# Attention with decay and a gated convolution FFN: the cleaning of q and k for half batches 4 to 7 on GpSimd instead of VectorE

## The chip, the cores and the metric

The kernel runs on one core of a Trainium2 chip. The metric is the device time of one execution in microseconds; the time before is the median of three runs. The core has TensorE (PE), with its weight loads shown as an engine of their own (PEld), VectorE (DVE), ScalarE (ACT), GpSimd (POOL) and SyncE (SP), whose queue (SPq in the profile) issues nearly all DMAs of this kernel.

## The reference, cut to what matters

Eight batches of eight heads, sequence 576, head size 64; attention with a decay per position, then a gated convolution FFN of width 1024.

```python
scores = q @ k.T / 8                       # per batch and head
cum    = cumsum(log(clip(f, 1e-4, 1)))
scores = where(causal, -1e9, scores + cum[:, None] - cum[None, :])
x      = softmax(scores) @ v               # heads side by side: 8 x 576 x 512
h      = relu(x @ w_in)                    # 8 x 576 x 1024
conv   = sum over k of conv_w[k] * h shifted by k - 1
out    = (h * sigmoid(conv)) @ w_out
```

## The kernel before, in words

The work is cut in 16 half batches (hb) of four heads each, and in 8 batches (b) for the FFN. q and k are wanted with the head size on partitions. They are loaded as 16-bit halves of the 32-bit numbers, so that 64 float32 give 128 partitions of bfloat16: the odd partitions hold the upper halves, which are the bfloat16 values wanted, and the even ones hold the lower halves, which have to be overwritten. For half batches 0 and 1 TensorE turns a plain load; from 2 on a transposing DMA from SP's queue does it (`load_qk`, L224, the DMA on L227), one for q and one for k, each 128x2304 in a ring of four tiles `qk`.

For half batches 2 to 7 a *clamp* cleans the tile in place (`clamp`, L231, the instruction on L233): each element, read as uint16, is multiplied by a factor of its partition (1 on odd, 0 on even ones) and a constant of its partition is added, which puts a bfloat16 1 or -1 or a zero in the rows that serve the decay. Then `rows_of` (L246, DMAs on L249 and L250, from SP's queue) writes the rows of cumulated decay into even partitions 0, 2 and 4, and TensorE can make the scores. From half batch 8 on DMAs (`fill`, L240) do all of it and no clamp is needed.

The scores of a half batch are made in PSUM by TensorE (L359, with the decay riding on the even rows), ScalarE takes the exponentials (L400, L417, L379), TensorE multiplies with v (L436, L441), VectorE divides by the sums (`norm`: L449, L450, reading PSUM), TensorE turns the result (L458, L459) and VectorE or ScalarE copies it out of PSUM (L464). In the FFN of a batch, per block of 128 channels: TensorE (L473), ScalarE's relu (L483), two scalar_tensor_tensor of VectorE for the convolution (L488, L490), ScalarE's tanh (L493), VectorE's gate, a third scalar_tensor_tensor (L497); then TensorE's second matmul (L504, L508), a copy out of PSUM (L514, L519) and the store (L525, L530, L534). GpSimd casts part of v (`cast_v`, L264 and L266) and of the weights (L552), issues a few DMAs for constants (`zc`, L330 and L331) and masks the exponentials of half batches 8 to 15 (L382, L403).

All tasks have names, and the order is written out by hand in one long string, ORDER: `Plan.play` emits the tasks in that order, and every engine and every queue works through its own in that order. Names: `q5.0` is the load of q for half batch 5 (`.1` is k), `cl5.0` its clamp, `rw5` the two row DMAs, `sd`, `so`, `st` scores, `ed`, `eo`, `et` exponentials, `pv` the product with v, `n` norm, `t` and `tx` the turn and its copy, `va` the cast of v, `wo1` and `woc1` the load and cast of a quarter of w_out, `f`, `r`, `c`, `d`, `a`, `g`, `o`, `e`, `s` the steps of the FFN; `@` names the engine where a task can run on several. A clamp depends on its load (`q`); `rw` depends on both clamps. Around the change the string reads (before; parts left out):

```python
"... q5.0 so4.1 g0.1 va3.0@DVE q5.1 ... d0.5 cl5.0 a0.2 so7.1 ... cl5.1 n2.0 q4.1 d0.3 va3.1@POOL eo7.0 wo2 rw5 ..."
"... woc2@POOL g0.2 so6.0 cl4.1 eo6.0 q4.0 f0.7 ... q6.0 n3.0 ... cl4.0 rw4 wo3 ... v2.0 ... cl6.0 g0.7 q6.1 ..."
"... woc3@POOL o0.0 g1.0 eo8.0 cl6.1 ... q7.0 cl7.0 v2.4 so8.1 va5.1@POOL ... rw6 q7.1 ... zc ... cl7.1 ... rw7 ..."
```

Of the kernel before, what the change touches and what calls it, by code (L numbers as in the profile page):

```python
# [25 lines left out]
so7.1 ed7 eo7.1 pv2.0 so7.0 va2.1@DVE pv2.1 cl5.1 n2.0 q4.1 d0.3 va3.1@POOL eo7.0 wo2 rw5 so6.1 eo6.1 woc2@POOL g0.2
so6.0 cl4.1 eo6.0 q4.0 f0.7 r0.7 wo0 woc1@ACT pv3.0 a0.3 a0.5 n2.1 t2 q6.0 n3.0 tx2@ACT c0.7 g0.5 pv3.1 n3.1 a0.4 g0.3
sd11 ed11 so11.1 eo11.1 sd10 so10.1 eo10.1 ed10 cl4.0 rw4 wo3 woc0@ACT t3 tx3@DVE f1.0 r1.0 d0.7 a0.7 c0.6 d0.6 a0.6
f1.1 r1.1 f1.2 g0.4 so11.0 c1.0 v2.0 d1.0 sd8 f1.3 g0.6 r1.2 eo11.0 ed8 cl6.0 g0.7 q6.1 v2.2 r1.3 sd9 ed9 c1.3 d1.3
so8.0 v2.1 f1.4 r1.4 c1.4 d1.4 h1 a1.0 woc3@POOL o0.0 g1.0 eo8.0 cl6.1 st5 et5 a1.4 c1.1 g1.4 d1.1 so10.0 eo10.0 f1.5  # L30
a1.3 g1.3 so9.1 eo9.1 v2.3 va5.0@DVE r1.5 c1.5 d1.5 o0.1 e0.0@ACT f1.6 r1.6 f1.7 r1.7 st4 so9.0 eo9.0 a1.1 va4.0@DVE
pv5.0 q7.0 cl7.0 v2.4 so8.1 va5.1@POOL pv5.1 et4 eo8.1 rw6 q7.1 va4.1@ACT n5.0 sd13 v3.0 v3.4 pv4.0 n5.1 pv4.1 ed13 zc
n4.0 n4.1 a1.5 v3.1 so13.1 sd12 eo13.1 cl7.1 ed12 c1.2 t5 so12.0 eo12.0 t4 tx4@ACT tx5@ACT o0.2 q9.0 c1.7 d1.7 so12.1
eo12.1 a1.7 rw7 o0.3 c1.6 e0.1@ACT f2.0 f2.1 d1.2 d1.6 so13.0 a1.2 g1.5 g1.7 r2.0 f2.2 f2.3 r2.1 q8.1 eo13.0 g1.2 c2.0
st7 a1.6 o0.4 r2.3 g1.1 v3.2 v3.3 q9.1 et7 sd15 d2.0 r2.2 h2 c2.1 a2.0 e0.2@DVE so15.0 so15.1 ed15 g1.6 eo15.0 sd14
ed14 so14.0 eo14.0 f2.4 r2.4 f2.5 va6.0@POOL pv6.0 c2.3 d2.3 q8.0 c2.2 g2.0 so14.1 r2.5 o1.0 eo15.1 va7.0@DVE
va7.1@ACT d2.2 c2.4 st6 eo14.1 pv7.0 a2.2 et6 va6.1@DVE n6.0 pv6.1 d2.1 a2.1 d2.4 n7.0 v4.0 fi9 s0.2 v4.1 c2.5 s0.0
v4.4 fi8 q10.0 s0.1 a2.4 v4.3 n6.1 v4.2 g2.2 o1.1 e1.0@ACT pv7.1 sd19 f2.6 f2.7 q11.0 q10.1 g2.4 ed19 n7.1 r2.6 c2.6
d2.6 r2.7 sd18 ed18 t6 q11.1 t7 o1.2 tx6@DVE tx7@ACT a2.6 a2.3 d2.5 a2.5 g2.1 st9 f3.0 et9 g2.3 f3.1 so19.1 c2.7 d2.7
r3.0 r3.1 a2.7 md19 sd17 ed17 o1.3 f3.2 g2.6 g2.5 c3.0 so19.0 eo19.1 e1.1@DVE r3.2 eo19.0 d3.0 c3.2 o1.4 e1.2@DVE s1.2  # L40
c3.1 d3.1 md18 st8 s1.0 g2.7 fi10 so18.0 fi11 et8 f3.3 va9.0@DVE va9.1@ACT md17 s1.1 v5.0 eo18.0 so17.0 so18.1 h3 d3.2
a3.0 r3.3 eo17.0 a3.1 f3.4 f3.5 f3.6 g3.1 v5.3 v5.1 r3.5 g3.0 o2.0 a3.2 g3.2 c3.3 r3.4 r3.6 sd16 f3.7 eo18.1 mt8 ed16
so16.1 eo16.1 r3.7 d3.3 a3.3 c3.4 d3.4 v5.2 c3.7 d3.7 c3.6 so16.0 eo16.0 o2.1 e2.0@ACT a3.4 pv9.0 a3.7 va8.0@ACT
so17.1 q12.0 n9.0 md16 va8.1@ACT q12.1 eo17.1 o2.2 o2.3 e2.1@ACT st10 et10 c3.5 d3.5 d3.6 mt9 g3.4 pv9.1 n9.1 mt10
pv8.0 pv8.1 a3.5 n8.0 a3.6 n8.1 o2.4 g3.7 q13.0 g3.5 v5.4 e2.2@ACT fi12 s2.2 sd22 ed22 sd20 ed20 md22 t8 tx8@DVE t9
tx9@DVE g3.6 g3.3 q13.1 so20.0 md20 sd23 so22.1 eo20.0 ed23 sd21 md23 va11.0@DVE ed21 f4.0 r4.0 c4.0 d4.0 f4.1 f4.2
r4.1 eo22.1 f4.3 c4.1 r4.2 r4.3 so23.1 eo23.1 h4 so21.1 d4.1 a4.0 g4.0 so23.0 f4.4 r4.4 eo21.1 c4.2 a4.1 s2.1 o3.0
eo23.0 f4.5 v6.0 r4.5 f4.6 d4.2 a4.2 so22.0 md21 g4.1 fi13 eo22.0 c4.4 va11.1@DVE st11 et11 s2.0 mt11 o3.1 c4.5 d4.5
v6.3 so21.0 r4.6 o3.2 v6.1 v6.2 a4.5 so20.1 q14.1 q14.0 eo21.0 e3.0@ACT d4.4 f4.7 eo20.1 c4.6 g4.5 r4.7 sd24 a4.4
pv11.0 ed24 sd25 o3.3 c4.3 d4.3 g4.2 c4.7 d4.7 so25.1 md24 n11.0 pv11.1 ed25 e3.1@ACT va10.0@POOL eo25.1 a4.7 pv10.0  # L50
st12 d4.6 va10.1@POOL pv10.1 et12 sd27 n11.1 n10.0 n10.1 ed27 g4.7 o3.4 t10 e3.2@ACT a4.6 a4.3 t11 sd26 tx10@DVE
tx11@DVE md27 v6.4 ed26 so25.0 so27.1 g4.6 eo27.1 f5.0 f5.1 so26.0 q15.0 r5.0 c5.0 g4.3 d5.0 eo25.0 r5.1 c5.1 f5.2
so24.0 eo26.0 f5.3 f5.4 r5.2 eo24.0 r5.3 g4.4 o4.0 so26.1 so27.0 h5 a5.0 fi14 d5.1 a5.1 r5.4 eo27.0 c5.3 g5.0 d5.3
eo26.1 c5.4 c5.2 s3.2 q15.1 d5.2 so24.1 d5.4 eo24.1 a5.2 g5.1 va12.0@DVE o4.1 f5.5 st13 et13 va12.1@ACT g5.2 f5.6 md25
mt12 md26 r5.5 c5.5 d5.5 f5.7 r5.6 sd28 e4.0@ACT r5.7 c5.7 ed28 pv12.0 n12.0 so28.1 o4.2 pv12.1 a5.5 g5.5 va13.0@ACT
pv13.0 eo28.1 d5.7 a5.3 mt13 sd29 s3.0 md28 o4.3 va13.1@POOL n12.1 ed29 md29 c5.6 n13.0 fi15 pv13.1 a5.4 g5.4 e4.1@ACT
s4.1 n13.1 sd31 ed31 md31 sd30 t12 ed30 d5.6 md30 t13 o4.4 a5.6 tx12@DVE tx13@DVE so31.0 st14 a5.7 g5.6 g5.3 f6.0 et14
mt14 v7.0 eo31.0 r6.0 c6.0 f6.1 r6.1 c6.1 d6.0 f6.2 r6.2 e4.2@ACT so31.1 eo31.1 f6.3 so29.0 so29.1 g5.7 f6.4 r6.3 c6.2
d6.1 d6.2 eo29.0 r6.4 v7.2 c6.4 eo29.1 d6.4 o5.0 so28.0 o5.1 s4.0 h6 a6.1 eo28.0 g6.1 a6.2 st15 f6.5 v7.3 a6.0
e5.0@ACT et15 mt15 s3.1 c6.3 v7.1 va14.0@DVE pv14.0 v7.4 so30.0 s4.2 g6.0 g6.2 r6.5 va15.0@POOL va15.1@ACT eo30.0  # L60
n14.0 so30.1 c6.5 eo30.1 f6.6 r6.6 f6.7 va14.1@POOL pv14.1 d6.5 a6.4 d6.3 n14.1 a6.3 pv15.0 pv15.1 t14 r6.7 c6.6 a6.5
o5.2 n15.0 n15.1 t15 tx14@ACT tx15@ACT c6.7 d6.7 a6.7 d6.6 o5.3 g6.3 g6.7 e5.1@ACT f7.0 f7.1 r7.0 f7.2 o5.4 g6.4 f7.3
g6.5 a6.6 r7.1 c7.0 d7.0 r7.2 e5.2@ACT r7.3 c7.1 d7.1 h7 a7.0 g6.6 c7.2 d7.2 f7.4 f7.5 f7.6 f7.7 g7.0 a7.1 g7.1 r7.6
r7.4 s5.2 o6.0 o6.1 o7.0.0 c7.6 c7.3 r7.5 d7.3 d7.6 a7.2 c7.4 d7.4 a7.3 e6.0@ACT s5.0 g7.3 c7.5 a7.4 g7.2 o6.2 o6.3
o6.4 r7.7 c7.7 d7.5 g7.4 s6.0 o7.2.0 o7.3.0 o7.0.1 o7.0.2 a7.6 o7.2.1 o7.1.0 o7.2.2 e6.1@ACT d7.7 o7.2.3 s5.1 o7.1.1
o7.3.1 o7.1.2 o7.1.3 e6.2@ACT o7.0.3 o7.1.4 o7.2.4 a7.5 g7.6 g7.5 o7.2.5 a7.7 s6.2 s6.1 g7.7 o7.1.5 o7.2.6 o7.2.7
e7.2@ACT s7.2 o7.0.4 o7.0.5 o7.0.6 o7.0.7 o7.1.6 o7.3.2 o7.1.7 e7.0@ACT s7.0 e7.1@DVE o7.3.3 o7.3.4 o7.3.5 o7.3.6
o7.3.7 e7.3@ACT o7.4.0 o7.4.1 o7.4.2 s7.1 o7.4.3 o7.4.4 o7.4.5 s7.3 o7.4.6 o7.4.7 e7.4@ACT s7.4
"""


# [35 lines left out]
def kernel(  # L107
# [11 lines left out]
    nc = tc.nc  # L119
# [34 lines left out]
    cw = cpool.tile([128, NFF, 3], FP32, name="cw")  # L154
    cwt = cpool.tile([128, NFF, 3], FP32, name="cwt")
# [3 lines left out]
    lim = cpool.tile([128, 4], FP32, name="lim")  # L159
# [33 lines left out]
    add = plan.add  # L193
# [34 lines left out]
            t.bitcast(U16)[:, h0 * S:(h0 + nh) * S],  # L228
            src[hb // 2, HH * (hb % 2) + h0:HH * (hb % 2) + h0 + nh].bitcast(U16).rearrange("h s d2 -> (h s) d2"))

    def clamp(hb, h0, nh, side):  # L231
        t = (stq_t, stk_t)[side][hb % RING].bitcast(U16)[:, h0 * S:(h0 + nh) * S]
        nc.vector.tensor_scalar(t, t, lim[:, 2 * side:2 * side + 1], lim[:, 2 * side + 1:2 * side + 2],  # L233
                                op0=ALU.mult, op1=ALU.add)

    def even_rows(hb, first, n, c0, c1):
        t, width = qk_t[hb % RING], 2 * HS + 64
# [50 lines left out]
    for side in range(2):  # L288
# [6 lines left out]
                            op0=ALU.is_equal, op1=ALU.mult)  # L295
# [274 lines left out]
    for hb in range(NHB):  # L570
# [146 lines left out]
```

## Time and profile before

| | |
|---|---|
| median of three runs | 249.03 us (248.84 to 250.57) |
| the profiled execution | 250.38 us |
| its span, and what lies around it | 248.4 us, 2.0 us |
| busy: PE, VectorE, ScalarE, GpSimd | 232.6, 215.3, 213.0, 46.2 us |
| L233 on VectorE | 12 times, 10.5 us, 874 ns each, from 17.7 to 85.3 us |
| L488, L490, L497 on VectorE | 64 times each, mean 832, 852, 806 ns |
| granted TensorE clock | 0.999 |

Busy time is a union of the instructions of an engine. Consecutive instructions overlap a little in the records: a VectorE instruction of 0.87 us is followed by the next after 0.79 us. A name such as "DVE u L490" is engine, written tile and line; SPq is SyncE's queue, which issues a DMA and then goes on. The chain of waits follows the end of the program back through whatever released each step.

### The profile page before, as it was taken

Reading aid. Unit: us, or ns where it says so; the run is one execution under the profiler, and the core shown is the slowest. Engines: PE = TensorE matmul, PEld = TensorE weight load, DVE = VectorE, ACT = ScalarE, POOL = GpSimd, SP = SyncE. Lnnn points to the kernel's source line nnn. Section 1 sums busy time; section 2 is a strip of 40 time slices with the busy share of each in tenths; the row PEclk is TensorE's granted clock in tenths of the full one; section 3 lists DMA queues with packets and bytes.
Section 4 is the critical chain, followed back from the end, with each engine's and each line's share of the span. In section 5 each row is a group of like instructions: output and inputs, shape, how many; then the busy total and the mean of one; then the engine's idle time right before and its main releaser. Section 6 shows DMA issues by size and latency. Waiting matters only on the chain.

```text
span 248.4 us, 6681 instructions
## 1 busy us (share of the span) xinstructions
PE 232.6 (94%) x2768; PEld 150.9 (61%) x2768; DVE 215.3 (87%) x328; ACT 213.0 (86%) x288; POOL 46.2 (19%) x76
## 2 busy tenths in 40 slices
PE   0999989889999999999999999999999999999993
PEld 0887765556456856666555865587556756755441
DVE  5771577998999989989999999997999999999961
ACT  2868938999999999969999899998999999887642
POOL 8000411101104302011203080046012602000000
PEclk9999999999999999999999999999999999999999
DMA  7989999999998999999999989899970690003345
GB/s 198 302 193 193 239 211 231 186 271 203 247 212 180 235 198 250 268 219 218 218 261 253 216 174 268 224 235 160 220 229 5 163 305 2 3 3 106 129 145 191
DMA packets 114694, 48.22 MB, mean 194 GB/s; under 512 B 104034, under 2 KB 105250, under 8 KB 114664
## 3 DMA queue, kind: packets, MB, share of 16 engines
q1 hardware_dynamic: 114210, 46.92, 85.1%
q8 instruction: 21, 0.34, 0.6%
q0 software_dynamic: 208, 0.51, 0.6%
q10 hardware_dynamic: 246, 0.37, 0.5%
q14 instruction: 9, 0.07, 0.1%
HBM read 21.11 MB, written 10.17 MB: 126 GB/s over the span
## 4 chain that ended last, share of the span: by engine, by line
PE 65%; SPq 9%; DVE 9%; DMA 8%; ACT 3%; issue 3%; ACTq 0%; DVEq 0%
PE ps L504 21%; PE ps L473 19%; PE ps L359 11%; SPq L227 6%; PE ps L436 6%; DMA qk<-in_k_dram 3%; PE ps L508 3%; DVE u L488 3%; DMA qk<-in_q_dram 3%; DVE u L490 2%; DMA u<-in_f_dram 2%; PE ps L458 2%; PE ps L441 2%; DVE hg L497 2%; DVE qk L233 1%
## 5 line engine op out<-in xcount | busy, mean ns | idle before, releaser
L417 ACT ACTIVATE pp<-ps 128x1024 f16<-128x1024 f32 x64 | 65.5, 1044 | 4.9 <-PE ps L359 2.7
L473 PE MATMUL ps<-xt,w_in_f 128*128 128x512 f16 (+1 forms) x512 | 68.2, 286 | 1.0 <-ACT ht L483 0.3
L359 PE MATMUL ps<-qk 128*128 128x128 bf16 (+2 forms) x576 | 63.2, 240 | 1.7 <-DVE xm L450 0.6
L504 PE MATMUL ps<-w_out_f,hg 128*128 128x512 f16 x256 | 59.4, 379 | 0.0
L488 DVE SCALAR_TENSOR_TENSOR u<-ht,cwt 128x576 f32<-128x576 f16 x64 | 52.8, 832 | 2.5 <-ACT ht L483 2.4
L490 DVE SCALAR_TENSOR_TENSOR u<-ht,cwt,u 128x576 f32<-128x576 f16 x64 | 53.7, 852 | 1.4
L473 PEld LDWEIGHTS <-w_in_f 128*128 128x128 f16 x512 | 34.0, 98 | 30.4 <-issue 1.8
L493 ACT ACTIVATE hg<-u,cw 128x576 f16<-128x576 f32 x64 | 48.8, 784 | 2.9 <-DVE u L490 2.9
L497 DVE SCALAR_TENSOR_TENSOR hg<-hg,ht 128x576 f16<-128x576 f16 x64 | 50.3, 806 | 1.1 <-ACT hg L493 0.9
L359 PEld LDWEIGHTS <-qk 128*128 128x128 bf16 x576 | 39.2, 98 | 19.2 <-issue 3.4
L483 ACT ACTIVATE ht<-ps 128x576 f16<-128x576 f32 x64 | 41.2, 668 | 2.9 <-PE ps L473 2.8
L504 PEld LDWEIGHTS <-hg 128*128 128x128 f16 x256 | 24.0, 98 | 25.6 <-issue 0.2
L403 POOL TENSOR_SCALAR_AFFINE_SELECT pp<-pd 128x1024 f16<-128x1024 f32 x16 | 18.5, 1168 | 48.7 <-ACT pd L400 42.9
L450 DVE TENSOR_TENSOR xm<-ps,rc 128x896 f16<-128x896 f32 (+1 forms) x32 | 24.3, 758 | 1.1
L436 PE MATMUL ps<-va,pp 128*128 128x65 f16 x640 | 24.6, 193 | 0.6 <-ACT pp L417 0.4
L436 PEld LDWEIGHTS <-pp 128*128 128x128 f16 x640 | 22.4, 97 | 3.0 <-ACT pp L417 0.7
L400 ACT ACTIVATE pp<-ps 128x1024 f16<-128x1024 f32 x16 | 16.5, 1039 | 4.0 <-PE ps L359 3.0
L514 ACT COPY ob<-ps 128x1024 f32<-128x1024 f32 (+1 forms) x18 | 15.1, 839 | 4.0 <-PE ps L504 3.2
L400 ACT ACTIVATE pd<-ps 128x1024 f32<-128x1024 f32 x16 | 15.9, 1023 | 1.9 <-PE ps L359 1.9
L367 PE MATMUL ps<-mask,ident 128*128 128x512 bf16 (+1 forms) x40 | 14.5, 362 | 0.4 <-ACT xt L464 0.2
L233 DVE TENSOR_SCALAR qk<-qk,lim 128x2304 uint16<-128x2304 uint16 x12 | 10.5, 874 | 3.1 <-DMA qk<-in_q_dram 1.9
L382 POOL TENSOR_SCALAR_AFFINE_SELECT pt<-p 128x256 f16<-128x256 f32 x8 | 4.8, 594 | 38.6 <-ACT p L379 37.0
(88 smaller groups left out, 198.9 us busy)
## 6 DMA issues: line engine op xcount, KB each, us to landing
vf<-in_v_dram SPq DMA_DIRECT2D x32, 256.0 KB, 4.9
out_dram<-ob SPq DMA_DIRECT2D x14, 512.0 KB, 4.7
qk<-blank SPq DMA_DIRECT2D x8, 540.0 KB, 7.2
ob<-in_moe_w_in_dram SPq DMA_DIRECT2D x4, 512.0 KB, 4.8
ob<-in_moe_w_out_dram SPq DMA_DIRECT2D x4, 512.0 KB, 5.1
vf<-in_v_dram SPq DMA_DIRECT2D x8, 128.0 KB, 5.0
out_dram<-ob SPq DMA_DIRECT2D x4, 256.0 KB, 2.1
out_dram<-ob SPq DMA_DIRECT2D x15, 64.0 KB
```

The source lines that it names most:

```text
L359: nc.tensor.matmul(o, tk[:, h * S + k0:h * S + k0 + 128], tq[:, h * S + q0:h * S + q0 + n], start=first, stop=last and not by_matmul(hb, h))
L400: nc.scalar.activation(o, ps_of(f"sd{i}").rearrange("p (s c) -> p s c", s=2), AF.Exp, scale=SCALE)
L417: nc.scalar.activation(pair(i)[:, s, 512:1536], ps_of(f"so{i}.{s}"), AF.Exp, scale=SCALE)
L436: nc.tensor.matmul(ps[:, c:c + D + 1], block(hb, h, m, n), va[:, h, m, 0:D + 1], start=(m == 0), stop=(m == n))
L450: nc.vector.tensor_tensor(xm[:, CUT * D * u:CUT * D * u + nj * k * D].rearrange("p (j x d) -> p j x d", x=k, d=D), got[:, :, :, 0:D], r.un ...
L473: nc.tensor.matmul(ps[:, t0:t1], w_in_f16[:, cc, 128 * ff:128 * (ff + 1)], xt[:, cc, x:x + t1 - t0], start=(cc == 0), stop=(cc == NCC - 1))
L483: nc.scalar.activation(ht_of(b, ff)[:, 1:1 + S], ps_of(f"f{b}.{ff}")[:, 0:S], AF.Relu, scale=0.5)
L488: nc.vector.scalar_tensor_tensor(u, ht[:, 0:S], cwt[:, ff, 0:1], ht[:, 1:1 + S], op0=ALU.mult, op1=ALU.add)
L490: nc.vector.scalar_tensor_tensor(u, ht[:, 2:2 + S], cwt[:, ff, 1:2], u, op0=ALU.mult, op1=ALU.add)
L493: nc.scalar.activation(hg_of(b, ff), u_t[slot[f"c{b}.{ff}", "u"]], AF.Tanh, scale=cw[:, ff, 1:2])
L497: nc.vector.scalar_tensor_tensor(hv, hv, 1.0, ht_of(b, ff)[:, 1:1 + S], op0=ALU.add, op1=ALU.mult)
L504: nc.tensor.matmul(ps[:, 512 * (c % 2):512 * (c % 2 + 1)], hg_of(b, ff)[:, 128 * c:128 * (c + 1)], w_out_f16[:, ff, :], **kw)
```

## The change

The tasks `cl4` to `cl7`, two each, run on GpSimd; `cl2` and `cl3` stay on VectorE. `clamp` gets an engine, the tasks `cl2` to `cl7` may run on either, and eight names in ORDER get `@POOL`. No name changes its place in the string. ORDER is written on one line after the change, so lines of the changed kernel are numbered 50 lower (L233 becomes L183, L249 becomes L199).

```diff
 ORDER = """
-... d0.5 cl5.0 a0.2 so7.1 ed7 eo7.1 pv2.0 so7.0 va2.1@DVE pv2.1 cl5.1 n2.0 q4.1 d0.3 va3.1@POOL ...
+... d0.5 cl5.0@POOL a0.2 so7.1 ed7 eo7.1 pv2.0 so7.0 va2.1@DVE pv2.1 cl5.1@POOL n2.0 q4.1 d0.3 va3.1@POOL ...
...
-    def clamp(hb, h0, nh, side):
+    def clamp(hb, h0, nh, side, e="DVE"):
         t = (stq_t, stk_t)[side][hb % RING].bitcast(U16)[:, h0 * S:(h0 + nh) * S]
-        nc.vector.tensor_scalar(t, t, lim[:, 2 * side:2 * side + 1], lim[:, 2 * side + 1:2 * side + 2],
-                                op0=ALU.mult, op1=ALU.add)
+        (nc.gpsimd if e == "POOL" else nc.vector).tensor_scalar(t, t, lim[:, 2 * side:2 * side + 1], lim[:, 2 * side + 1:2 * side + 2],
+                                                                op0=ALU.mult, op1=ALU.add)
...
-                    add(f"cl{hb}.{side}", "DVE", [f"q{hb}.{side}"], lambda hb=hb, side=side: clamp(hb, 0, 4, side))
+                    add(f"cl{hb}.{side}", "DVE/POOL", [f"q{hb}.{side}"], lambda e, hb=hb, side=side: clamp(hb, 0, 4, side, e))
```

(`cl4.0`, `cl4.1`, `cl6.0`, `cl6.1`, `cl7.0` and `cl7.1` get `@POOL` in the same way.)

In GpSimd's own order the eight clamps stand so: wic2, cl5.0, cl5.1, va3.1, woc2, cl4.1, cl4.0, cl6.0, woc3, cl6.1, cl7.0, va5.1, zc, cl7.1, va6.0, and then as before. The row DMAs `rw4` to `rw7` on SP's queue and the first scores of half batches 4 to 7 on TensorE wait for GpSimd where they waited for VectorE. VectorE loses eight instructions; the order of all other engines' instructions is the same.

## The prediction

> **What bounds the kernel now.** The page comes first: the engines' busy times and the chain that ended last.
>
> ```profile
> PE 232.6 (94%) x2768; PEld 150.9 (61%) x2768; DVE 215.3 (87%) x328; ACT 213.0 (86%) x288; POOL 46.2 (19%) x76
> ...
> PE 65%; SPq 9%; DVE 9%; DMA 8%; ACT 3%; issue 3%; ACTq 0%; DVEq 0%
> ```
>
> On average TensorE is the limit and POOL nearly idle. But the eight moved instructions run between 50.66 and 86.17 us, so that stretch must be read by itself: busy time by window (columns: PE, PEld, DVE, ACT, POOL, granted clock, DMA share, GB/s).
>
> ```profile
> 45.00:50.00 5.00, 3.87 (x42) 2.68 (x42) 4.96 (x8) 5.00 (x8) 0.09 (x1) 1.00 1.21 199
> 50.00:55.00 5.00, 4.01 (x72) 2.90 (x73) 4.97 (x9) 4.99 (x7) 0.00 (x0) 1.00 1.04 250
> ...
> 65.00:70.00 5.00, 4.69 (x46) 2.88 (x44) 4.96 (x7) 5.00 (x9) 1.04 (x1) 1.00 1.10 277
> ...
> 75.00:80.00 5.00, 5.00 (x66) 3.14 (x65) 4.96 (x8) 5.00 (x8) 2.00 (x4) 1.00 0.82 168
> ```
>
> Here VectorE and ScalarE are both full, and PE waits for them up to 75 us; from there PE has no gap. Third, the chain of waits in that stretch (start, us, what).
>
> ```profile
> 49.93 0.81 DVE u L490
> 50.74 0.52 DVE qk L233
> ...
> 53.81 0.55 SPq L250
> 54.36 0.05 issue
> 54.41 6.86 DMA qk<-in_q_dram
> 61.27 0.03 issue
> 61.30 0.46 DVE qk L233
> ...
> 72.74 0.83 DVE u L490
> 73.60 0.78 ACT hg L493
> ```
>
> From 38.4 to 73.6 us the chain is VectorE, but for one transposing load (54.41 to 61.27) on which VectorE waits 0.59 us; then ScalarE to 81.3, then PE to the end. So a microsecond added to VectorE before 73.6 goes to the end whole, while one taken away helps only until ScalarE binds.
>
> Fourth, the timeline of VectorE and GpSimd where they overlap (start, us; VectorE first, GpSimd in the second fence).
>
> ```profile
> 39.21 0.81 DVE L488 SCALAR_TENSOR_TENSOR u<-ht,cwt 128x576 f32<-128x576 f16 x1
> 40.12 1.40 DVE L490 SCALAR_TENSOR_TENSOR u<-ht,cwt,u 128x576 f32<-128x576 f16 x1
> ...
> 67.31 1.62 DVE L497 SCALAR_TENSOR_TENSOR hg<-hg,ht 128x576 f16<-128x576 f16 x1
> ```
> ```profile
> 39.83 1.09 POOL L552 CAST w_in_f<-ob 128x1024 f16<-128x1024 f32 x1 [4.04 <-DMA ob<-in_moe_w_in_dram]
> 44.41 0.68 POOL L266 CAST va<-vf 64x256 f16<-64x256 f32 x1 [3.49 <-DMA vf<-in_v_dram]
> ...
> 67.29 1.04 POOL L552 CAST w_out_f<-ob 128x1024 f16<-128x1024 f32 x1 [9.37 <-DMA ob<-in_moe_w_out_dram]
> ```
>
> These rows decide the forecast. L490 takes 0.82 us elsewhere and 1.40 when it begins under a GpSimd cast; L497 takes 0.75 elsewhere and 1.62 under the cast of 67.29, which ends at 68.33: its own 0.75 starts only at 68.18. The other way round, the cast of 44.41 (0.39 us alone, at 188.89) takes 0.68 because L490 runs until 44.84. So a GpSimd instruction that reads SBUF and a VectorE scalar_tensor_tensor exclude each other: GpSimd gets in 0.15 us before the running VectorE instruction's recorded end, and the next scalar_tensor_tensor starts about 0.2 us before GpSimd's end. VectorE's PSUM readers are free of it: L450 under the cast of 56.88 takes 1.09, as without one (52.71).
>
> **The change, part by part.**
>
> *Removed:* eight VectorE L233 instructions of 0.87 us, 0.79 us from start to next start. Five (cl5.0, cl5.1, cl4.1, cl4.0, cl6.0) stand before the last work of the chain's VectorE part: 5 x 0.79 = 3.95 us. With cl4.0 goes the wait for its load at 61.30, 0.68 us (L497 at 59.95 and its usual spacing of 0.67 give 60.62), and VectorE's 0.19 us wait for PE at 56.72, since VectorE will be later: 0.87 us. In all -4.82 us.
>
> *Added on GpSimd:* eight tensor_scalar on 128x2304 uint16, an operation that this engine does not show. Nearest rows: the 128x1024 cast takes 1.04 us, so by proportion 2.34; from the 64x256 cast (0.39) the slope is 0.846 ns per element, 0.39 + 2048 x 0.000846 = 2.12; the 128x1024 affine_select (1.10) by proportion 2.48. I take 2.34 (same proportion as the larger, single-input cast). Ends: 2.12, and 4.68 if multiply and add each cost a pass.
>
> *Added on VectorE, the exclusion:* a clamp that arrives while scalar_tensor_tensors run back to back holds VectorE 2.34 - 0.28 = 2.06 us (mean of the replay below). Followed by hand from 48.74, with landing times of the loads:
> - cl5.0 lands at 48.74, gets in at 49.01 before L488's end, ends 51.36; L490 (49.20) begins at 51.16: +1.96.
> - cl5.1 (landed 50.62) gets in behind that L490 at 51.83, ends 54.18; the second L490: +2.07.
> - Then va3.1, queued behind cl5.1 on POOL (44.41 before, now 54.65): +0.15 on L266. Its user pv3.1 comes at about 59, so nothing else.
> - woc2 (56.88), which lay under L450, now falls on L490/L497: +0.79.
> - cl4.1 lands at 54.79 but stands behind woc2: 58.43 to 60.78, mostly under L449/L450: +0.16.
> - cl4.0: its load is issued 0.83 us later, since SP's rw5 (L249, 53.40) waits for cl5.1's end at 54.18 instead of 53.35. It lands near 62.1, holds to 64.45, the last L497 before tx2 waits +1.73.
> - cl6.0 (lands near 65.5): +2.06. cl6.1 (near 73.8, since SP's rw4 now waits for 64.45 instead of 62.65, 1.8 us, with wo3, v2, q6.1 and later loads behind it): +2.08.
> Sum 1.96 + 2.07 + 0.15 + 0.79 + 0.16 + 1.73 + 2.06 + 2.08 = +11.00 us.
>
> *After 73.6:* cl7.0 holds about 2.06 more for 2 x 0.79 removed, cl7.1 comes behind zc's DMA issues (78.62 to 82.69) and holds at most 2.06 more for the last 0.79. VectorE is then up to 1.75 us further behind; I cost that at nothing, covered by VectorE's slack against PE after 86 (4.31 of 5 us busy in 90 to 95); without that cover it is +1.7. At best it is nothing: ScalarE and PE, not VectorE, are then the chain. rw6 and rw7 wait for nothing new: cl6.1 and cl7.1 end ahead of SP's shifted queue. POOL's zc (needed by the fill at 98.39) has over 10 us.
>
> *Sum:* 11.00 - 4.82 = **+6.2 us**. The profiled execution took 250.38 (span 248.4 and 1.98 around it), so it would be 256.6; it lies 1.35 above the median 249.03, which would be **255.2**. By the ends of the clamp's price, with 4.85 fully exposed clamps: 2.12 gives 255.2 - 4.85 x 0.22 = 254.1; 4.68 gives 255.2 + 4.85 x 2.34 = 266.5, and near 270 with the covered ones.
>
> A page to weigh: the row of L497 shows all but 0.15 us of a GpSimd cast held. The Trainium skill, SBUF — State Buffer, "Who interferes with whom", says a VectorE instruction with two SBUF inputs and a GpSimd one that reads SBUF take turns on a shared port pair, whichever starts first keeping it for the whole instruction. By its letter each hold would be the full 2.34 and the sum 255.2 + 4.85 x 0.28 = 256.6.
>
> **Rivals.**
> 1. *The clamp is slower on GpSimd* (two operations and a conversion). For: the row is missing. Against: every GpSimd row, even affine_select, is near 1 ns per element. At 3.44 us each (proportion of the cast at 95.68, which takes 1.53 beside VectorE work) 255.2 + 5.9 x 1.10 = 261.7 (cl4.1 loses its cover too); at 4.68, 266 to 270. The Trainium skill, GPSIMD Engine Reference, "Elementwise — side-by-side cycle accounting", gives 1.8 cycles per element at 1.2 GHz as the best case of a plain loop, an estimate of 3.46 us here; the cast row (1024 in 1.04) is faster than that.
> 2. *The holds are covered* (the other side: no change or faster). It decides at a hold where 4.85 h + 1.1 = 4.82, so 0.77 us, a clamp of about 1.05 us: less than half of any POOL row; or if uint16 tensor_scalar does not exclude at all. Then VectorE sheds 4.8 us, but ScalarE, full from 45 to 70, gives only its gaps, 0.3 us up to 80 us (0.31 of it between 70 and 75): 248.7. If other waits vanish too, PE's gaps between 35 and 75 (3.5 us) cap it at 245.5.
> 3. *The wait goes to SP instead* (no exclusion, but rw4 waits): cl4.0 ends 61.27 + 2.34 = 63.61 instead of 62.65 as SP's time, and all loads behind come 1.0 us later: 249.0 + 1.0 = 250.0. For: SP is issuing almost without a gap from 45 to 80. Against: it is less than what VectorE loses.
> 4. *Half absorbed:* VectorE's lateness meets slack between 73.6 and 81 that the single chain doesn't show (PE full from 75): 252.
>
> **How the numbers follow.** Forecast as summed 0.52 (its own range 253 to 259, from 254.1 and 256.6 widened by the uncounted 1.7 and by one hold more or less); slower clamp 0.20; half absorbed 0.13; SP 0.06; covered 0.09. The 8-in-10 range leaves out the covered case (0.09) and the upper half of the slow clamp (0.10): 250 to 265. A measurement here tells about 1% (2.5 us) from no change: slower by more, above 251.5, is 0.52 + 0.20 + 0.10 of the absorbed case = 0.82; faster by over 1% only in the best part of the covered case, 0.04; within 1% the rest, 0.14.
>
> **What would show it.** In the profile after: L183 on POOL x8 near 2.3 us each (lines are 50 lower there); VectorE's three scalar_tensor_tensor groups (832, 852, 806 ns) longer by some 13 us in sum; single ones of 2.8 us next to each clamp; VectorE's busy time up, though it lost 7 us of work; PE's gaps between 50 and 85 grown by about 6 us; after 86 us windows as before. Wrong it would be if those groups keep their means (no exclusion), if L183 on POOL is far from 2.3, or if the chain runs through SP's L199 and POOL instead of VectorE.

## The result and the profile after

The changed kernel takes 258.99 us (median of four runs, 258.65 to 259.24) where the kernel before took 249.80 us in the same comparison (248.84 to 250.58): a ratio of 1.0365 [1.0338, 1.0392], slower by 9.2 us. The forecast was 255.2 with a range of 250 to 265, so the sign and the range hold and the size is 3.8 us short (as a difference 3.0 short, 9.2 instead of 6.2, since the kernel before is at 249.80 here and was at 249.03). The profiled execution took 258.65 us against 250.38. Executions of one kernel below can differ by stretches of 3.41 us or more at half TensorE clock; where that matters they are given one by one with their mean granted clock.

The page first, engines and the chain that ended last.

```profile
PE 234.3 (91%) x2768; PEld 152.0 (59%) x2768; DVE 224.5 (87%) x320; ACT 213.6 (83%) x288; POOL 66.9 (26%) x84
...
PE 68%; DVE 14%; DMA 5%; SPq 4%; ACT 3%; issue 2%; ACTq 0%; DVEq 0%
```

VectorE has eight instructions less and is busy 9.2 us longer; its share of the chain goes from 9% to 14%, that of SP's queue falls from 9% to 4%. The groups of the same page say which instructions grew (busy, mean ns of one, idle before).

```profile
L440 DVE SCALAR_TENSOR_TENSOR u<-ht,cwt,u 128x576 f32<-128x576 f16 x64 | 59.2, 937 | 1.4
...
L438 DVE SCALAR_TENSOR_TENSOR u<-ht,cwt 128x576 f32<-128x576 f16 x64 | 57.3, 903 | 2.6 <-ACT ht L433 2.4
...
L447 DVE SCALAR_TENSOR_TENSOR hg<-hg,ht 128x576 f16<-128x576 f16 x64 | 52.1, 835 | 1.3 <-ACT hg L443 1.1
...
L183 POOL TENSOR_SCALAR qk<-qk,lim 128x2304 uint16<-128x2304 uint16 x8 | 21.0, 2630 | 17.7 <-DMA qk<-in_q_dram 15.8
```

The three scalar_tensor_tensors of the convolution (852, 832, 806 ns before, in this order) are longer by 64 x (85 + 71 + 29) ns = 11.8 us in sum; nothing about them was changed. The clamp's mean of 2630 ns includes waiting for VectorE; one that starts free takes 2.26 us. Single instructions show the hold: VectorE's timeline (start, us), then GpSimd's.

```profile
48.67 3.44 DVE L440 SCALAR_TENSOR_TENSOR u<-ht,cwt,u 128x576 f32<-128x576 f16 x2
52.04 2.19 DVE L216 CAST va<-vf 64x256 f16<-64x256 f32 x1
...
65.87 2.62 DVE L440 SCALAR_TENSOR_TENSOR u<-ht,cwt,u 128x576 f32<-128x576 f16 x1
72.28 2.62 DVE L440 SCALAR_TENSOR_TENSOR u<-ht,cwt,u 128x576 f32<-128x576 f16 x1
...
79.52 2.66 DVE L447 SCALAR_TENSOR_TENSOR hg<-hg,ht 128x576 f16<-128x576 f16 x1
...
85.64 3.10 DVE L438 SCALAR_TENSOR_TENSOR u<-ht,cwt 128x576 f32<-128x576 f16 x1
```
```profile
71.31 2.98 POOL L183 TENSOR_SCALAR qk<-qk,lim 128x2304 uint16<-128x2304 uint16 x1 [1.93 <-DMA qk<-in_k_dram]
...
85.86 2.26 POOL L183 TENSOR_SCALAR qk<-qk,lim 128x2304 uint16<-128x2304 uint16 x1
```

The clamp of 85.86 ends at 88.12; the L438 recorded from 85.64 needs 0.81 and ends at 88.74, so it starts work about 87.93, 0.2 us before the clamp's recorded end. At 52.04 it is not a scalar_tensor_tensor but VectorE's cast of v that is held, 2.19 us instead of 0.28. Summed over VectorE between 46 and 93 us, the time beyond each kind's median is 1.0 us in the kernel before and 14.3 us after. This sum is called *held time* below.

By window (PE, PEld, DVE, ACT, POOL, granted clock, DMA share, GB/s):

```profile
50.00:55.00 5.00, 2.63 (x60) 2.08 (x58) 4.97 (x5) 3.19 (x4) 4.48 (x3) 0.91 1.06 293
55.00:60.00 5.00, 5.00 (x78) 3.52 (x78) 4.02 (x7) 3.81 (x5) 3.97 (x3) 0.75 0.93 179
...
65.00:70.00 5.00, 4.50 (x40) 2.49 (x38) 4.80 (x3) 3.82 (x5) 3.76 (x2) 1.00 1.08 253
70.00:75.00 5.00, 2.76 (x25) 1.69 (x25) 4.94 (x5) 3.68 (x5) 2.98 (x1) 1.00 1.23 220
75.00:80.00 5.00, 3.90 (x29) 2.01 (x27) 4.82 (x7) 4.31 (x7) 1.28 (x1) 1.00 1.04 128
...
85.00:90.00 5.00, 3.59 (x77) 2.68 (x75) 4.96 (x5) 4.60 (x7) 3.09 (x3) 1.00 1.21 229
```

ScalarE was full from 45 to 70 and has gaps now; PE, which had 0.1 us of them from 75 to 95, has them up to 90.3 us; and between 54.06 and 57.47 PE ran at half clock. PE's own shift (the same instruction before and after) tells when the time is lost: about -0.5 us at 46, +2.6 at 55, +3.0 at 62, +5.1 at 67, +6.3 at 73, +6.9 at 79, +8.1 at 82, and +8.3 from 83 (times of before) to the end. The chain of waits in that stretch:

```profile
51.30 0.81 DVE u L440
52.12 2.12 DVE va L216
...
54.28 0.54 PE ps L391 x12
...
79.60 2.58 DVE hg L447
...
85.72 3.04 DVE u L438
...
90.39 1.10 DVE xm L400
...
91.53 0.41 PE ps L386 x8
```

VectorE carries it to 91.5 us, not to 73.6. Two of PE's waits there (window 48 to 92; us in total, times, longest) were not in the forecast:

```profile
PE ps L391 <- DVE va L216: 2.2, 1, 2.2
PE ps L386 <- DVE va L214: 1.7, 2, 1.2
```

A third wait, 2.3 us for ScalarE's relu (L433, PE stands from 69.93 to 72.24), brought no half clock. For GpSimd or a row DMA PE waits nowhere in this window.

### The profile page after: what moved, and what is told of

It is laid out like the page before. It is cut to its first block, busy times and chain, and to the rows that moved or that the text cites. A ratio compares the mean times of both kernels' runs of the same rounds, so it can differ in the third digit from the quotient of the medians.

```text
span 256.9 us, 6686 instructions
## 1 busy us (share of the span) xinstructions
PE 234.3 (91%) x2768; PEld 152.0 (59%) x2768; DVE 224.5 (87%) x320; ACT 213.6 (83%) x288; POOL 66.9 (26%) x84
## 4 chain that ended last, share of the span: by engine, by line
PE 68%; DVE 14%; DMA 5%; SPq 4%; ACT 3%; issue 2%; ACTq 0%; DVEq 0%
PE ps L454 20%; PE ps L423 19%; PE ps L309 12%; PE ps L386 6%; DVE u L438 4%; DVE u L440 4%; DMA qk<-in_k_dram 3%; PE ps L458 3%; PE ps L408 2%; PE ps L391 2%; DVE hg L447 2%; SPq L177 2%; PE ps L163 2%; DMA pd<-in_moe_conv_w_dram 2%; ACT ht L433 1%
## 5 line engine op out<-in xcount | busy, mean ns | idle before, releaser
L309 PE MATMUL ps<-qk 128*128 128x128 bf16 (+2 forms) x576 | 64.5, 242 | 2.0 <-DVE xm L400 0.8
L440 DVE SCALAR_TENSOR_TENSOR u<-ht,cwt,u 128x576 f32<-128x576 f16 x64 | 59.2, 937 | 1.4
L438 DVE SCALAR_TENSOR_TENSOR u<-ht,cwt 128x576 f32<-128x576 f16 x64 | 57.3, 903 | 2.6 <-ACT ht L433 2.4
L447 DVE SCALAR_TENSOR_TENSOR hg<-hg,ht 128x576 f16<-128x576 f16 x64 | 52.1, 835 | 1.3 <-ACT hg L443 1.1
L433 ACT ACTIVATE ht<-ps 128x576 f16<-128x576 f32 x64 | 41.1, 664 | 4.7 <-PE ps L423 3.1
L386 PE MATMUL ps<-va,pp 128*128 128x65 f16 x640 | 24.6, 193 | 2.4 <-DVE va L214 1.7
L183 POOL TENSOR_SCALAR qk<-qk,lim 128x2304 uint16<-128x2304 uint16 x8 | 21.0, 2630 | 17.7 <-DMA qk<-in_q_dram 15.8
L386 PEld LDWEIGHTS <-pp 128*128 128x128 f16 x640 | 22.3, 97 | 5.1 <-DVE va L214 2.1
L400 DVE TENSOR_TENSOR xm<-ps,rc 128x896 f16<-128x896 f32 (+1 forms) x32 | 24.3, 758 | 1.1
```

The source lines that it names most:

```text
L309: nc.tensor.matmul(o, tk[:, h * S + k0:h * S + k0 + 128], tq[:, h * S + q0:h * S + q0 + n], start=first, stop=last and not by_matmul(hb, h))
L386: nc.tensor.matmul(ps[:, c:c + D + 1], block(hb, h, m, n), va[:, h, m, 0:D + 1], start=(m == 0), stop=(m == n))
L400: nc.vector.tensor_tensor(xm[:, CUT * D * u:CUT * D * u + nj * k * D].rearrange("p (j x d) -> p j x d", x=k, d=D), got[:, :, :, 0:D], r.un ...
L433: nc.scalar.activation(ht_of(b, ff)[:, 1:1 + S], ps_of(f"f{b}.{ff}")[:, 0:S], AF.Relu, scale=0.5)
L438: nc.vector.scalar_tensor_tensor(u, ht[:, 0:S], cwt[:, ff, 0:1], ht[:, 1:1 + S], op0=ALU.mult, op1=ALU.add)
L440: nc.vector.scalar_tensor_tensor(u, ht[:, 2:2 + S], cwt[:, ff, 1:2], u, op0=ALU.mult, op1=ALU.add)
```

## The experiments

Three mechanisms could make the 9 us. **A, exclusion:** GpSimd's clamp, which reads SBUF, keeps VectorE out. **B, lateness:** what waits for the clamps, or stands behind them in GpSimd's order, comes later, since 2.26 us on GpSimd replace 0.87 on VectorE. **C, clock:** PE's new gaps bring half clock. Each ratio is to the kernel before, run beside it.

### The same place and the same waits, without reading SBUF

`e1_memset`; a memset of the tile takes the place of GpSimd's clamp, so q and k of half batches 4 to 7 are zero.

```diff
-        (nc.gpsimd if e == "POOL" else nc.vector).tensor_scalar(t, t, ...)
+        if e == "POOL":
+            nc.gpsimd.memset(t, 0)
+        else:
+            nc.vector.tensor_scalar(t, t, ...)
```

> The eight GpSimd clamps become memsets of the same 128x2304 uint16 tile: same place, same waits, about the same length (the 64x1152 memset of before takes 1.13 us, so by proportion 2.26, as against 2.26 for an undisturbed clamp), but nothing is read from SBUF. Left out: the cleaning, so q and k of half batches 4 to 7 are zero. Theory A (a GpSimd instruction that reads SBUF and a two-input VectorE instruction exclude each other): the holds of some 14.8 us are gone, VectorE's three scalar_tensor_tensor groups are back at about 830, 850, 806 ns, and the time is 248 to 250, as before the change. Theory B (the rows and scores wait for a later clamp, on SP's queue and on TensorE): the clamps end no earlier, so the time stays near 259.

Measured 250.95 us, ratio 1.0027 [0.9993, 1.0061]. Groups of its page (lines are 3 higher than after):

```profile
L441 DVE SCALAR_TENSOR_TENSOR u<-ht,cwt 128x576 f32<-128x576 f16 x64 | 53.2, 839 | 3.8 <-ACT ht L436 3.7
L443 DVE SCALAR_TENSOR_TENSOR u<-ht,cwt,u 128x576 f32<-128x576 f16 x64 | 54.3, 862 | 1.4
...
L450 DVE SCALAR_TENSOR_TENSOR hg<-hg,ht 128x576 f16<-128x576 f16 x64 | 49.1, 787 | 1.8 <-ACT hg L446 1.6
...
L184 POOL MEMSET qk<- 128x2304 uint16 x8 | 16.2, 2036 | 19.3 <-ACT pp L370 8.1
```

GpSimd is occupied 2.04 us each time, nearly as long as by the clamp, and the convolution keeps its length. Held time is 2.2 us. So at this length neither the place in the order nor the new wait costs the 9 us; what the clamp does and the memset doesn't is the cause. (The operation differs too, not the read alone; but GpSimd's casts, which read and neither multiply nor add, hold the same instructions.)

`e6_memset_short`; the same bytes zeroed as 1152 float32, so that GpSimd is done in half the time (cleaning left out as before):

```diff
+            nc.gpsimd.memset((stq_t, stk_t)[side][hb % RING].bitcast(FP32)[:, 0:HS // 2], 0.0)
```

> As the run with memsets, but each memset is written as 128x1152 float32 (the same bytes), so about 1.05 instead of 2.03 us. Left out: the cleaning, q and k of half batches 4 to 7 are zero. No hold, hardly any lateness: this shows what the 6.3 us taken from VectorE are worth alone. Rival 2 of the prediction said 248.7 against 249.03, a gain of 0.3 us, since ScalarE is full. If lateness had hidden a real gain in the run with memsets of 2.03 us, this one is 2 to 4 us under the kernel before, 247 to 248.5.

Measured 249.91 us, 0.9973 [0.9956, 0.999]: the memset takes 1.06 us, held time is 1.0 as before the change. Taking the clamps off VectorE and giving back nothing is worth 0.7 us [0.3, 1.1], although it sheds 8 x 0.79 = 6.3 us of VectorE's work. By this run that is about what the change could have brought.

### The exclusion with nobody waiting

`e7_idle_read`; the kernel before, whose VectorE keeps its clamps; GpSimd cleans a spare tile that nothing else uses, at each one's place in GpSimd's order (with no load to wait for, the first starts at 41.75).

```diff
     def clamp(hb, h0, nh, side):
+        if hb >= 4:
+            nc.gpsimd.tensor_scalar(spare, spare, lim[:, 0:1], lim[:, 1:2], op0=ALU.mult, op1=ALU.add)
```

> The kernel before, all clamps on VectorE, and eight tensor_scalar of 128x2304 uint16 added on GpSimd in a spare tile, at the clamps' places in the order; nobody waits for their results. Theory A: about 2 us of hold for each that falls beside two-input instructions, nothing saved in exchange; 8 to 14 us over before, 258 to 264, and longer scalar_tensor_tensor groups. Theory B (only the wait for a late clamp costs): no change, 250 to 251.

Measured 262.62 us, 1.0485 [1.0423, 1.0547] (executions 261.6 to 265.3). From its page:

```profile
L494 DVE SCALAR_TENSOR_TENSOR u<-ht,cwt,u 128x576 f32<-128x576 f16 x64 | 58.9, 933 | 1.4
...
L492 DVE SCALAR_TENSOR_TENSOR u<-ht,cwt 128x576 f32<-128x576 f16 x64 | 55.2, 870 | 2.5 <-ACT ht L487 2.4
...
L501 DVE SCALAR_TENSOR_TENSOR hg<-hg,ht 128x576 f16<-128x576 f16 x64 | 54.2, 868 | 1.0 <-ACT hg L497 0.7
...
L237 POOL TENSOR_SCALAR spare<-spare,lim 128x2304 uint16<-128x2304 uint16 x8 | 24.6, 3077 | 0.4
```

No engine waits for the spare tile, the clamps are where they were, and PE waits for no GpSimd instruction between 40 and 95 us, yet held time is 12.4 us and the kernel 11.9 us longer, with half clock for 3.41 us from 70.20 on, behind a PE gap of 1.97 us. A, with what its gaps bring, makes a loss of this size without B. With e1 beside it, A is shown as the cause from which the rest follows.

`e8_idle_write`; as e7, but GpSimd only writes the spare tile.

```diff
     def clamp(hb, h0, nh, side):
+        if hb >= 4:
+            nc.gpsimd.memset(spare, 0)
```

> The same with eight memsets of the spare tile (2.03 us each) in place of the eight tensor_scalar: GpSimd as busy and its queue as long, but nothing read from SBUF. Theory A: no change, 250 to 251.5, and VectorE's groups keep their means. If it is a busy GpSimd as such or its queue that costs, it is as slow as the run with tensor_scalar.

Executions of 251.25 (clock 0.999), 256.83, 256.88 and 257.68 us (0.993): my expectation of no change holds for one of four. The scalar_tensor_tensors are indeed free (835, 851, 816 ns), but VectorE's clamp is not. Its timeline, then GpSimd's:

```profile
82.22 2.39 DVE L267 CAST va<-vf 128x1024 f16<-128x1024 f32 x1
84.53 2.65 DVE L234 TENSOR_SCALAR qk<-qk,lim 128x2304 uint16<-128x2304 uint16 x1
```
```profile
84.08 2.48 POOL L237 MEMSET spare<- 128x2304 uint16 x1
```

The clamp L234 (0.88 alone) runs to 87.18 because the memset holds it to 86.56. The cast before it (0.69 alone) lies under GpSimd's DMA issues of `zc`, which end at 84.09; why it is held there is not shown. Held time is 6.4 us, 5.2 of them on this cast and three of VectorE's clamps. The clamp of 84.53 and the cast before it delay PE, which stands from 85.84 to 88.50 and has half clock from 88.32 on for 3.41 us. So "write only" is not harmless for every VectorE instruction. It was harmless in e1 for the scalar_tensor_tensors; there too one cast (2.15 us instead of 0.69, under the memset of 80.12 to 82.14) is the exception. The Trainium skill, SBUF — State Buffer, "Who interferes with whom", separates these two: two SBUF inputs contend with a GpSimd instruction that reads, while tensor_scalar and cast in a two-port mode contend with any. Both halves agree with the rows (839 against 903 ns; 2.65 against 0.88 us).

### Half of the change, and one clamp of it

`e3_hb45` keeps cl5.0, cl5.1, cl4.1 and cl4.0 on GpSimd, `e4_hb67` the four of half batches 6 and 7, `e11_cl71` cl7.1 alone.

```diff
-... cl6.0@POOL ... cl6.1@POOL ... cl7.0@POOL ... cl7.1@POOL
+... cl6.0@DVE ... cl6.1@DVE ... cl7.0@DVE ... cl7.1@DVE
```

(e4: the same with cl4 and cl5; e11: seven names with `@DVE`.)

> Only half batches 4 and 5 are cleaned on GpSimd; 6 and 7 stay on VectorE. Theory A, by the holds read in the trace after the change (1.89, 1.91, 0.84 and 1.42 us, less 4 x 0.79 of VectorE work and the 0.9 us wait for a load): +2 to +3, so about 252. Theory B: SP's two late rows (rw5, rw4) are both here, so nearly all of the loss, 257 to 259. Theory C (TensorE's granted clock, 0.91 and 0.75 of full from 50 to 60 us after the change, adds much): the dip is here, and the loss is above 4 us.

> Only half batches 6 and 7 are cleaned on GpSimd. Theory A, by the holds read in the trace after the change (1.80, 1.80, 1.91, 2.29, less 4 x 0.79): +4.6 to +5.5, so about 254.5; the last two alone +2.5, since VectorE has no room behind 73.6 us as I had assumed. Theory B: rw6 and rw7 waited for nothing new, so 250 or less. Theory C: no clock dip from 50 to 60, and what is missing from the sum of both halves is the clock's share.

> One clamp alone on GpSimd: cl7.1, whose load lands at 82.6 while VectorE reads PSUM (L449, L450 from 81.4 to 85.3). Theory A: no hold at all, VectorE sheds 0.79 us, GpSimd's clamp takes its bare 2.26 us; the time is that of before or up to 0.5 us less, 250.2 to 250.8. If a clamp on GpSimd costs wherever it stands, about an eighth of the loss, 1.1 us more.

| | us | ratio | held time | held time added, less VectorE's work removed | time added |
|---|---|---|---|---|---|
| e3 | 252.3 | 1.0074 [1.0045, 1.0102] | 6.4 | 6.42 - 1.01 - 4 x 0.79 = +2.2 | +1.9 |
| e4 | 254.31 | 1.0153 [1.009, 1.0216] | 6.5 | +2.3 | +3.8 |
| all eight | 258.99 | 1.0365 [1.0338, 1.0392] | 14.3 | 14.33 - 1.01 - 8 x 0.79 = +7.0 | +9.2 |
| e11 | 250.63 | 1.001 [0.9989, 1.0031] | 3.6 | | +0.3 |

Each half costs, and the second half, two of whose clamps the forecast put behind the end of VectorE's chain, costs more than the first by the middle values (the intervals just touch). Together they cost 3.5 us more than the sum of the two. 2.4 of these are held time itself (14.33 against 6.42 + 6.50 - 1.01), the rest may be room used only once and the half clock, which neither profile of the halves has. e4's ratio is of its three executions without half clock (253.52, 254.16, 254.46); a fourth took 259.21 (clock 0.993). In e11 the one clamp was to fall on VectorE's readers of PSUM; it came later (85.95) and held an L438 by 1.8 us (86.20, 2.61 long), and still costs nothing that can be measured. PE's shift against the kernel before is 1.0 us ahead of this hold and 0.9 behind it: one hold there fits in VectorE's room.

### Lateness by itself

`e2_memset_twice`; e1 with the memset twice, so GpSimd is occupied 4.1 us for each clamp without reading.

```diff
+            for _ in range(2):
+                nc.gpsimd.memset(t, 0)
```

> As the run with memsets, but each memset is done twice, so a clamp ends some 2.3 us later still, without reading SBUF. Left out: the cleaning. Theory A with rows that have room: 249 to 251, for only what SP's queue waits at rw5 and rw4 is added, and it is taken up by gaps. Theory B: each late clamp costs, so the time is well above the run with single memsets, by 4 us or more, and over 259.

Measured 258.26 us, 1.0298 [1.0228, 1.0369]. Held time is only 2.7 us, so this loss is another one. Its chain of waits, then PE's waits (window 60 to 95):

```profile
84.03 2.44 POOL qk L185
86.47 0.35 POOL va L220
...
86.87 0.54 PE ps L395 x12
```
```profile
PE ps L395 <- POOL va L220: 3.6, 1, 3.6
PE ps L313 <- DMA qk<-image: 1.7, 1, 1.7
```

The longest wait is not for a cleaned tile but for va5.1, a 0.35 us cast that stands behind cl7.0 in GpSimd's order; PE stands from 83.26 to 86.87, and half clock is granted from 85.48 on for 6.83 us. The rows behind the late clamps cost too: PE waits for them from 67.29 to 68.95, the second line, and 1.1 us from 58.28 on. PE's shift against the kernel before is 2.3 us at 73 and 8.2 at 85, so most of the loss is the cast and the half clock. At 2.0 us per task (e1) the wait for the cast is 1.4 us and the time the same within its interval. B is real, then, with a threshold between 2 and 4 us per task.

`e5_quarters`; the clamp in four pieces of 128x576, so that VectorE gets in between.

```diff
+            for c in range(0, nh * S, S):
+                x = t[:, c:c + S]
+                nc.gpsimd.tensor_scalar(x, x, lim[:, 2 * side:2 * side + 1], ...)
```

> The eight clamps stay on GpSimd, each in four instructions of 128x576 (about 0.6 us each by proportion of 2.26). Theory A (exclusion): a hold is the GpSimd instruction less about 0.28 us, so a clamp's four holds would be 4 x 0.32 = 1.3 instead of 2.0 us and VectorE's excess falls from 14.3 to about 10 us; but GpSimd also has to wait for VectorE four times, so that a clamp takes 4 to 5 us from first to last. If the holds alone set the time: about 255. Theory B (lateness of the clamp counts as much): 258 or more, as in the run with two memsets each, whose clamps also end 2 us later.

Measured 260.76 us, 1.0403 [1.0345, 1.046]. Held time falls from 14.3 to 9.6 us, as A expects, and nothing is won: a quarter takes 0.82 us (not the fourth of 2.26), and with VectorE between the pieces eight of them in the first pair take 8.77 us (49.50 to 58.27). PE waits 3.8 us for GpSimd's casts of v behind them (L222), 1.3 for the cast of w_out and 1.3 for rows. Half clock comes twice: at 64.88, behind a wait of 2.2 us for VectorE's L406, and at 88.77, within the 3.2 us wait for a cast of v. So smaller pieces trade A for B.

### The clock, and the order

`e9_filled_gap`; after, with nine matmuls of no use where PE stands from 52.06 to 54.28.

```diff
+        if (hb, u) == (2, 1):
+            for _ in range(9):
+                nc.tensor.matmul(ps[:, 0:512], ident, w_in_f16[:, 0, 0:512], start=True, stop=True)
```

> The changed kernel with nine matmuls of 128x512 on constants put ahead of pv2.1 on TensorE, into PSUM that pv2.1 then overwrites: they fill the gap of 2.22 us (52.06 to 54.28 in the changed kernel's trace) in which TensorE waits for the held cast va2.1. In that trace the granted clock is 0.5 from 54.06 to 57.47 just behind the gap. Theory C (the gap costs a second time through the clock): no stretch of 0.5 there, and 1.0 to 1.7 us less than the changed kernel of the same job. Against it: the clock dips all the same, or the time stays, since VectorE and not TensorE sets the pace there.

Executions of 254.17 (clock 1.0), 255.78 (0.996), 258.88 (0.992) and 259.82 us (0.993), median 257.33; the ratio of the first two is 1.0174 [1.0115, 1.0233]. The windows of the profiled one, that of 258.88 us:

```profile
52.00:54.00 2.00, 2.00 (x17) 1.04 (x15) 1.97 (x4) 1.58 (x2) 2.00 (x2) 1.00 1.26 270
54.00:56.00 2.00, 2.00 (x38) 1.41 (x35) 2.00 (x2) 0.82 (x1) 1.51 (x2) 1.00 0.88 300
...
72.00:74.00 2.00, 2.00 (x14) 1.18 (x12) 1.37 (x3) 2.00 (x3) 1.04 (x1) 0.50 1.31 251
```

The half clock at 54 is gone with the gap. That the gap made it is not shown by this: in e12 (below) the same gap, 51.35 to 53.44, brought no half clock either. Another half clock follows a gap of 2.28 us (68.91 to 71.19). Held time is 13.6, nearly that of the change, but this is the execution of 258.88 us. The two near full clock, 1.7% or 4.4 us above the kernel before, have no profile, so they do not say what the same holds cost at full clock. Executions of one kernel with a mean clock of 0.993 or less lie above those near full clock by 4.4 us here, 5.2 in e4, 5.9 in e8 and 6.1 in e10 (below). A stretch of 3.41 us at half rate can take at most half of it, 1.7 us, so most of that distance is something else: the PE gaps, and holds that fall elsewhere.

`e12_after_again` is the changed kernel once more, and `e10_va21_early` the same with VectorE's cast va2.1 moved ahead of the clamps, so that no clamp holds it.

```diff
-... va3.0@DVE q5.1 ... so7.0 va2.1@DVE pv2.1 ...
+... va3.0@DVE va2.1@DVE q5.1 ... so7.0 pv2.1 ...
```

> The changed kernel with the task va2.1 (VectorE's cast that cl5.1 holds for 1.9 us, and that pv2.1 waits for) put ahead of the clamps' arrival, behind va3.0. Theory A + C: the hold falls on another VectorE instruction, but TensorE no longer waits for the cast, so the gap and the half clock go: 1.5 to 3 us less than the changed kernel, about 256.5. If only the sum of VectorE's holds counts: no change.

> The changed kernel once more, for comparison on the same chip: 259 within 1 us.

e12 gave 260.09 us, 1.038 [1.0336, 1.0425]. e10 gave 254.34 (clock 0.999), 260.21, 260.43 and 260.82 us (0.992 to 0.993): no gain that holds. The PE gap at 52 is gone, as expected, and does not decide. The profile of e10 is that of the 254.34 us, so the two can be set side by side where e12 loses most. VectorE's timeline of e12, then of e10:

```profile
84.14 4.16 DVE L438 SCALAR_TENSOR_TENSOR u<-ht,cwt 128x576 f32<-128x576 f16 x1
...
89.07 0.69 DVE L214 CAST va<-vf 128x1024 f16<-128x1024 f32 x1
```
```profile
87.94 1.09 DVE L400 TENSOR_TENSOR xm<-ps,rc 128x896 f16<-128x896 f32 x1
...
89.49 1.54 DVE L438 SCALAR_TENSOR_TENSOR u<-ht,cwt 128x576 f32<-128x576 f16 x2
```

GpSimd's cl7.1 lies from 85.42 to 87.68 in e12 and from 87.25 to 89.51 in e10. In e10 it falls on VectorE's readers of PSUM (L400: 1.09, its usual length) and holds nobody. In e12 it falls on L438, and the cast L214 behind that ends at 89.76, which PE waits for. The windows of e12, then of e10:

```profile
88.00:90.00 2.00, 0.19 (x4) 0.19 (x5) 1.93 (x5) 1.39 (x2) 0.00 (x0) 0.94 1.23 201
90.00:92.00 2.00, 2.00 (x40) 2.00 (x37) 1.69 (x4) 0.00 (x0) 0.00 (x0) 0.50 1.52 227
```
```profile
88.00:90.00 2.00, 2.00 (x40) 1.59 (x32) 1.97 (x4) 1.46 (x3) 1.51 (x1) 1.00 0.45 56
```

PE of e12 stands from 87.55 to 89.81 and has 3.41 us at 0.50 from 89.77 on; e10 loses nothing here. The lead of e10 grows from 0.99 us (at 84.28) to 3.42 (89.81), the gap, and to 4.81 (93.2), the clock, and stays there to the end. So 3.8 of the 4.8 us come here. Not all of that is where one clamp of eight falls: e12's L438 is recorded from 84.14, 1.3 us before the clamp began, while GpSimd issued the DMAs of `zc`, and 1.4 us are the half clock.

## Why the prediction was right, and where it failed

**The mechanism: right.** Shown by e7 (holds without waits for the clamps, +11.9 us) and e1 (the waits without the holds of the convolution, +0.2 us). The signs named came about: the three groups 11.8 us longer (13 forecast), single ones of 2.6 to 3.1 us next to five of the eight clamps, VectorE's busy time up, PE's idle time between 50 and 85 from 2.3 to 7.5 us (about 6 more forecast).

**The clamp's price: right.** 2.34 us was taken, 2.26 is measured free. Rival 1, the slow clamp, is out.

**The held time up to 73.6 us: near.** 11.00 us by the replay, 9.66 in the trace: cl5.0 +1.89, cl5.1 +1.91, woc2 +0.84, cl4.1 and cl4.0 together +1.42, cl6.0 and cl6.1 +1.80 each. One victim was wrong: behind cl5.0 a second L440 (51.30 to 52.12) passed the waiting cl5.1, which then held the cast va2.1. The forecast gave VectorE's casts +0.15, and did not see that PE's pv2.1 waits for this one.

**The waits that were to go, 0.87 us: not gained.** Both went, but VectorE now waits 0.9 us for PE's L386 at 59.20, just behind PE's half clock, and 0.6 for L409 at 65.19. Its idle time between 55 and 70 us is 1.62 us where it was 0.95. So 9.66 - 5 x 0.79 + 0.67 = 6.4 us, and PE's shift over that stretch is 6.8 (from -0.5 to +6.3): the forecast's 6.2 is nearly met by luck, because two errors, 1.3 and 1.5 us, cancel.

**The step that failed** is "I cost that at nothing, covered by VectorE's slack against PE after 86". cl7.0 holds an L447 by 1.91 and cl7.1 an L438 by 2.29 us. With the three last clamps removed from VectorE, 3 x 0.79, that leaves +1.8 us, and it goes to the end whole: the shift grows from 6.3 to 8.3. The forecast put the two holds in the wrong place. The clamps start near their old times (78.72 and 85.86; 80.66 and 85.30 before), but VectorE is 6 to 7 us late by then, so they fall on work that it did before at 73.48 and 78.34 (its timeline before):

```profile
73.48 0.75 DVE L497 SCALAR_TENSOR_TENSOR hg<-hg,ht 128x576 f16<-128x576 f16 x1
...
78.34 0.95 DVE L488 SCALAR_TENSOR_TENSOR u<-ht,cwt 128x576 f32<-128x576 f16 x1
...
80.05 0.69 DVE L264 CAST va<-vf 128x1024 f16<-128x1024 f32 x1
80.66 0.88 DVE L233 TENSOR_SCALAR qk<-qk,lim 128x2304 uint16<-128x2304 uint16 x1
```

The first of these stands right behind the last L490 of VectorE's part of the chain (72.74), and is itself in the chain after the change (79.60). Two places behind the second comes va4.0's cast (80.05 before, 89.51 after), for which PE waits at once: it stands from 89.05 to 90.26. The slack after 86 does exist for a VectorE that is not late: in e11 cl7.1 alone falls on an L438 at 86.20, holds it by 1.8 us and moves PE by nothing. The sign "after 86 us windows as before" fails by the clock (PE is busy 3.59 of 5 us from 85 to 90, where it was full), while the work that PE did from 83.2 us on before keeps its distance of 8.3. The price without that cover had been put at +1.7; it is +2.0. Rival 4, lateness half absorbed between 73.6 and 81, is out as well: the shift grows there from 6.3 to 6.9.

The sum is then 6.8 - 0.5 + 2.0 = 8.3 us between the two profiles. The profiled execution before lies 0.6 above its median in this comparison and the one after 0.3 below, which makes the 9.2.

**What no step had** is the half clock. In the profile after it takes 3.41 us from 54.06 on, in e12 3.41 us at 89.77. At half rate a full PE loses up to 1.7 us in such a stretch. Its price is smaller: in the profile after VectorE, which carries the chain there, waits 0.9 us for PE behind it, an estimate of the most that it costs; between e12 and e10 the shift grows by 1.4 across it. All eight executions of the changed kernel (after and e12) have a mean clock of 0.987 to 0.993, the two profiled ones with such a stretch each. That e9's 254.2 and 255.8 and e10's 254.34 lie near 255.2 does not confirm the forecast: they are other kernels, and they stand 3.9 to 5.5 us above the kernel before in their comparison, not 6.2.

**The other rivals.** Rival 2, covered holds, is the case of e1 and e6: no holds, 0.2 us more and 0.7 us less. Its 248.7 (0.3 us gained) was about right for that case, which the clamp's read excludes. Rival 3, SP: `rw5` waits on SP to 54.11 us for the end of cl5.1, as worked out (54.18), but `rw4`, `rw6` and `rw7` wait for nothing, and SP's queue has less of the chain than before.

**What stays open:** why the two halves add up to less than the whole in held time; why a gap brings half clock at one time and not at another; two profiles of the same kernel have their half clock at different places (54.06 and 89.77), so the 9.2 us can't be split to the tenth. By the 0.9 and 1.4 us above the half clock is the smaller part and the holds, with the PE gaps behind them, the larger. B alone costs nothing that can be measured for a task of 2.0 us (e1), and in the profile after PE waits for GpSimd nowhere from 48 to 92 us.

## What to carry to other kernels

Before work moves to GpSimd because VectorE is full, ask what VectorE runs beside it: here an instruction of 0.79 us became one that kept VectorE's two-input SBUF instructions, and some of its casts, out for 2 us. If it must move, put it under VectorE's readers of PSUM, and look at what stands behind it in GpSimd's own order. And place each hold by the order as the change shifts it: the moved instruction keeps the time of its load, while the held engine is already late, so the hold falls on earlier work than the old timeline says. Then follow the one instruction behind it to its reader.

## What the runs showed of the hardware that was not expected

- A GpSimd instruction that waits for VectorE does not always get the next turn. After cl5.0 a whole L440 of 0.81 us passed cl5.1 (51.30 to 52.12); in e3 a clamp recorded for 3.30 us was passed in the same way.
- A GpSimd memset, which reads nothing, left scalar_tensor_tensors alone (839 ns mean) and held VectorE's clamp (2.65 us instead of 0.88) and cast (2.15 instead of 0.69).
- The memset of 128x2304 16-bit elements takes 2.02 us, of the same bytes as 128x1152 float32 1.06 us: by elements, not bytes. The clamp in quarters, 0.82 us each, costs 45% more than whole.
- TensorE went to half clock for 3.41 us, or 6.83, in or behind gaps of only 1.97 to 3.61 us (after, e2, e5, e7, e8, e9, e12), and did not after others of 2.04 to 2.31 us (after at 69.93, e7 at 48.55, e9 at 88.26, e10 at 67.26, e12 at 51.35). The Trainium skill, TensorE: Matmul & The Clock Gate, Part 1, has the clock fall after at least one idle window of about 3.4 us; the length of the stretch agrees with its window of 3413 ns, the length of the gap that suffices does not.
- Three times VectorE was held while GpSimd was still recorded as issuing the DMAs of `zc` (e8's cast from 82.22; e9's L441 from 84.85, the clamp only from 86.13; e12's L438 from 84.14, the clamp only from 85.42). In the kernel before VectorE ran freely beside the same issues. The cause is not shown.
